# Nine output stores of a convolution move from ScalarE's instruction stream to SyncE's

## The chip, the cores and the metric

The kernel runs on one core of one Trainium2 chip. The metric is the device time of one launch, in microseconds (us). A core has a matrix engine (TensorE, PE in the profile), a vector engine (VectorE, DVE), an activation engine (ScalarE, ACT), a general engine (GpSimd, POOL) and SyncE (SP), which only issues transfers here. All five run their own instruction streams in order and meet at semaphores. Transfers (DMAs) are issued from SyncE, ScalarE or GpSimd, each of which has a queue of its own, and are carried out by 16 DMA engines.

## The reference

A causal convolution over 7 positions, with one softmax-normalised kernel per head, is followed by a mixture of experts with a capacity limit:

```python
# _attn_ref: x (8, 3584, 192), weight (8 heads, 7)
w = np.exp(weight - np.max(weight, axis=-1, keepdims=True))
w = w / (np.sum(w, axis=-1, keepdims=True) + 1e-09)
x_pad = np.concatenate([np.zeros((B, 6, D)), x], axis=1)
out = np.einsum('hk,bskhg->bshg', w, x_unf)        # 24 channels per head
# _moe_ref: N = 28672 tokens, D = 192, E = 8 experts, F = 1024, cap = N // E = 3584
logits = x @ w_gate
# tokens go to experts in falling order of logit, one expert each, while the expert has room
for e in range(E):
    mask = assigned == e
    out[mask] = np.maximum(x[mask] @ w1[e], 0.0) @ w2[e]
```

## The kernel before

The first stage, some 155 us, is the convolution. The input is cut into 16 *half batches* of 1792 positions. For each, `load` (line 183) brings the input into one of four buffers `X` of 118 partitions. It does so in three DMAs: the *head* (6 partitions, line 189 or 192), the *lower half* (112 partitions, 8 rows of 192 floats each, line 194 on SyncE) and the *upper half* (the same size, line 194 on ScalarE). SyncE issues the head and the lower half. The upper half is put on a list, `later`, and ScalarE issues it in the middle of a convolution, at the sixth of its eight heads. At the start of convolution i, `load(i + 3)` is written.

`conv` (line 202) does one half batch. For each of 8 heads TensorE multiplies the input by a banded matrix of the head's weights, into one of four PSUM banks `cv`, and ScalarE copies the bank to one of three output buffers `a`. This copy is called the eviction here. At the end the *store* (line 214) writes the output buffer, 1344 KB, to the array `attn` in the chip's memory. Before the change ScalarE issues it, at its place between the last eviction of one half batch and the first of the next.

The same half batch is then transposed by VectorE (`aT<-a`), TensorE forms the gate's logits from it (`pl`), ScalarE copies them out twice (`L<-pl`, `LT<-pt`), and VectorE takes the largest per token (`M<-LT`). This is one to two half batches behind the convolution. In between stand the steps of the routing, as a background list: a threshold search over the logits of the first half batches, then the counts and positions of the tokens of the first eight (half batches 0 to 7), among them a small copy on ScalarE called `tot`. From the lists that come out, GpSimd gathers the experts' first tokens from `attn`. The expert stage then runs to the end of the kernel, and TensorE has work for all of it.

The order of every engine's stream is fixed when the program is built. An estimate of the engines' progress (`Pace`, `Steps`) decides where the background steps are put; DMA issues count nothing in it. Waits are set by the builder, in two kinds that matter here:

- A wait for data or a free buffer: an eviction into `a` needs the store of three half batches earlier to have landed; a head needs TensorE to be done with the input of four half batches earlier.
- A wait for a semaphore. The DMAs of SyncE and ScalarE share eight completion semaphores (DMAHW0 to DMAHW7 in the listings), given out in turn. A DMA waits until the one that held its semaphore before has landed.

The routine of lines 1648 to 1680 is the loop over the half batches.

Of the kernel before, what the change touches and what calls it, by code (L numbers as in the profile page):

```python
# [114 lines left out]
def build(ctx, tc, nc, x, weight, wg, attn, LT, wk):  # L115
# [4 lines left out]
    V, A, PE, P = nc.vector, nc.scalar, nc.tensor, nc.gpsimd  # L120
# [81 lines left out]
    def conv(i, mid, hold=None):  # L202
        t = X.pop(i)
        a = AA[i] = k.ap[i % 3].tile([128, 16, D], F32, name="a")
        o = a.rearrange("p w (h c) -> p h w c", c=24)
        for h in range(8):
            ps = k.cps.tile([128, 512], F32, name="cv")
            PE.matmul(ps[:, 0:384], TH[0:118, h], t[:, :, h * 24:(h + 1) * 24], start=True, stop=True)
            mid(h)
            A.activation(o[:, h], ps[:, 0:384].rearrange("p (w c) -> p w c", c=24), AF.Copy)  # L210
        put = partial(A.dma_start, attn[i * 1792:(i + 1) * 1792].rearrange("(g p b) d -> p g (b d)", g=4, b=4),
                      a[0:W].rearrange("p (g b) d -> p g (b d)", b=4))
        if hold is None:
            put()  # L214
        else:
            hold.append(put)
# [24 lines left out]
    def logits_t(i):  # L241
# [5 lines left out]
        A.activation(o, v, AF.Copy)  # L247

    k.load, k.conv, k.transp, k.logits, k.logits_t = load, conv, transp, logits, logits_t
    k.toeplitz, k.gate_load, k.gate_ops = toeplitz, gate_load, gate_ops  # L250
    return k
# [1517 lines left out]
```

## Time and profile before

| | us |
|---|---|
| median of 3 runs (lowest to highest) | 1238.71 (1238.25 to 1239.27) |
| the profiled execution, whole | 1242.89 |
| its span | 1241.1 |
| TensorE busy in the span | 1203.0 (97%) |
| first store issued / last store issued | 21.23 / 156.44 |
| bytes moved by DMA over the span | 182.00 MB |

The profile is of one execution. Times in it count from the span's start. A row of a timeline gives the start, the length, the engine, the line, what is written from what, and in brackets how long the engine had stood idle before and what ended that wait. A row "ACTq" or "SPq" is the issue of a DMA by ScalarE or SyncE, not the transfer; its length is the time that the engine stood in it. Nearly all compute instructions pass through one helper, so their line is 56 and they are told apart by the names of their tiles.

### The profile page before, as it was taken

The numbers are of one execution on the slowest core, as the hardware profiler recorded it, in microseconds if no ns is written. First come the engines' busy times: TensorE is split into PE (matmuls) and PEld (weight loads), VectorE is DVE, ScalarE is ACT, GpSimd is POOL, SyncE is SP. The second block draws the span as 40 slices with busy tenths as digits, with TensorE's granted clock in tenths as the row PEclk, the third lists the DMA queues.
The fourth block names the chain that finished last, engine by engine and source line by source line (L and its number), as shares of the span: only waits on it lengthen the run. The fifth ranks groups of instructions, "written<-read, shape, count | busy, mean of one in ns | idle before, by whom it ended". The sixth has DMA issues, their size and how long they took to land.

```text
span 1241.1 us, 21785 instructions
## 1 busy us (share of the span) xinstructions
PE 1203.0 (97%) x7694; PEld 1033.9 (83%) x7694; DVE 984.8 (79%) x2126; ACT 559.6 (45%) x1251; POOL 532.5 (43%) x520
## 2 busy tenths in 40 slices
PE   6999899999999999999999999999999999999997
PEld 3545578889989988889888889999999999999996
DVE  7588679898998988889879856777777777777762
ACT  5544555556445454444554443343333433333332
POOL 2000234435556555555465435434544444543422
PEclk9999999999999999999999999999999999999999
DMA  9999664659427473745343442114223232423100
GB/s 249 369 347 325 202 215 121 151 159 323 140 68 215 134 244 83 255 155 184 102 130 105 126 106 70 45 39 158 94 100 105 100 101 93 155 69 125 48 24 28
DMA packets 128580, 182.00 MB, mean 147 GB/s; under 512 B 20992, under 2 KB 91088, under 8 KB 126800
## 3 DMA queue, kind: packets, MB, share of 16 engines
q1 hardware_dynamic: 85856, 104.13, 27.6%
q0 software_dynamic: 21504, 44.07, 12.0%
q10 hardware_dynamic: 21104, 32.34, 7.6%
q8 instruction: 62, 1.02, 0.3%
q14 instruction: 54, 0.44, 0.1%
HBM read 102.37 MB, written 78.12 MB: 145 GB/s over the span
## 4 chain that ended last, share of the span: by engine, by line
PE 87%; DVE 5%; DMA 4%; issue 1%; ACT 1%; ACTq 0%; SPq 0%; POOL 0%; POOLq 0%; DVEq 0%
PE ph L56 40%; PE y L56 39%; PE cv L56 4%; PE bg L56 3%; DMA attn<-a 3%; DVE X L56 1%; PE pl L56 1%; DVE TH L56 1%; DVE aT L56 1%; DVE hl L56 1%; DMA X<-otab 0%; PE px L56 0%; DMA wb<-in_weight_dram 0%; ACTq L214 0%; DMA otab<-X 0%
## 5 line engine op out<-in xcount | busy, mean ns | idle before, releaser
L56 PE MATMUL y<-w,hh 128*128 128x384 f32 x1792 | 535.7, 355 | 0.0
L56 ACT ACTIVATE hh<-ph 128x512 fp32r<-128x512 f32 x448 | 267.3, 597 | 453.1 <-PE ph L56 380.3
L56 PE MATMUL y<-w,hl 128*128 128x192 f32 x1792 | 448.9, 251 | 0.0
L56 DVE SCALAR_TENSOR_TENSOR hl<-ph,hh 128x512 fp32r<-128x512 f32 x448 | 307.6, 687 | 129.1 <-ACT hh L56 99.7
L56 PE MATMUL ph<-xa,w 128*128 128x512 f32 x1344 | 395.2, 402 | 0.4 <-DVE hl L56 0.4
L56 PEld LDWEIGHTS y<-w,hl 128*128 128x128 f32 x1792 | 340.9, 190 | 16.2
L56 PEld LDWEIGHTS y<-w,hh 128*128 128x128 f32 x1792 | 336.3, 188 | 20.9 <-issue 3.0
L1383 POOL DMA_INDIRECT out_dram<-yo,ia x128 | 144.3, 1127 | 240.2 <-DVE yo L56 195.7
L56 PEld LDWEIGHTS ph<-xa,w 128*128 128x128 f32 x1344 | 218.5, 189 | 21.6 <-issue 1.8
L1383 POOL DMA_INDIRECT out_dram<-yo,ib x96 | 94.9, 988 | 221.0 <-DVE yo L56 213.6
L56 PE MATMUL ph<-xd,w 128*128 128x512 f32 x448 | 177.3, 396 | 0.0
L1308 POOL DMA_INDIRECT xg<-attn,ja x128 | 141.5, 1106 | 78.9 <-issue 39.1
L56 PE MATMUL ph<-xd,dl 128*128 128x512 f32 x448 | 174.1, 389 | 0.2 <-issue 0.2
L56 DVE STREAM_TRANSPOSE xs<-xg 32x128 f32<-32x128 f32 (+2 forms) x408 | 164.8, 404 | 6.6
L56 ACT ACTIVATE yt<-y 128x192 f32<-128x192 f32 x224 | 73.0, 326 | 109.8 <-PE y L56 72.3
L56 DVE TENSOR_TENSOR yo<-y,yt 128x192 f32<-128x192 f32 x224 | 79.2, 354 | 49.9 <-ACT yt L56 46.6
L1308 POOL DMA_INDIRECT xg<-attn,jb x96 | 103.3, 1076 | 29.3 <-issue 29.3
L56 PE MATMUL cv<-X,TH 118*128 118x384 f32 x256 | 99.7, 516 | 13.9 <-DVE TH L56 12.2
L56 PEld LDWEIGHTS ph<-xd,dl 128*128 128x128 f32 x448 | 84.2, 188 | 20.1 <-issue 0.5
L56 PEld LDWEIGHTS ph<-xd,w 128*128 128x128 f32 x448 | 84.0, 187 | 19.6 <-issue 0.6
L56 PEld LDWEIGHTS cv<-X,TH 118*128 118x128 f32 x256 | 44.9, 195 | 43.7 <-POOL TH L152 12.0
L56 ACT ACTIVATE a<-cv 128x384 f32<-128x384 f32 x128 | 59.4, 493 | 43.1 <-PE cv L56 21.3
(237 smaller groups left out, 919.8 us busy)
## 6 DMA issues: line engine op xcount, KB each, us to landing
attn<-a ACTq DMA_DIRECT2D x16, 1344.0 KB
raw<-in_moe_w_dram SPq DMA_DIRECT2D x56, 192.0 KB
X<-in_x_dram SPq DMA_DIRECT2D x15, 672.0 KB
X<-in_x_dram ACTq DMA_DIRECT2D x15, 672.0 KB
kw<-w SPq DMA_DIRECT2D x36, 256.0 KB
kv<-w SPq DMA_DIRECT2D x24, 384.0 KB
scr<-xs SPq DMA_DIRECT2D x96, 96.0 KB
w<-kw SPq DMA_DIRECT2D x6, 1536.0 KB
```

Source lines behind the costliest of these rows:

```text
L56: return f(*a, **k)
L1308: self.nc.gpsimd.indirect_dma_start(out=t[:, b], out_offset=None, in_=self.attn[0:rows], in_offset=bass.IndirectOffsetOnAxis(ap=idx[b], ax ...
L1383: st = self.nc.gpsimd.indirect_dma_start(out=self.out, out_offset=bass.IndirectOffsetOnAxis(ap=idx, axis=0), in_=o, in_offset=None, bounds ...
```

## The change

The stores of half batches 0 to 8 are issued by SyncE and no longer by ScalarE. Those of 9 to 15 stay on ScalarE. What is stored, and from where, is the same.

```diff
@@ -208,7 +208,7 @@
             PE.matmul(ps[:, 0:384], TH[0:118, h], t[:, :, h * 24:(h + 1) * 24], start=True, stop=True)
             mid(h)
             A.activation(o[:, h], ps[:, 0:384].rearrange("p (w c) -> p w c", c=24), AF.Copy)
-        put = partial(A.dma_start, attn[i * 1792:(i + 1) * 1792].rearrange("(g p b) d -> p g (b d)", g=4, b=4),
+        put = partial((nc.sync if i < 9 else A).dma_start, attn[i * 1792:(i + 1) * 1792].rearrange("(g p b) d -> p g (b d)", g=4, b=4),
                       a[0:W].rearrange("p (g b) d -> p g (b d)", b=4))
         if hold is None:
             put()
```

The streams of TensorE, VectorE and GpSimd are the same in both programs. The first place is SyncE's stream while half batches 2 to 4 are convolved. X_451, X_519 and X_590 are the inputs of half batches 6, 7 and 8; a_387, a_455 and a_526 the outputs of 2, 3 and 4. Before:

```order
L189 DMA X_451<-in_x_dram 6x15x192 [waits DMAHW0_49,DMAHW5_49,PE_49,Pool_49]
L194 DMA X_451<-in_x_dram 112x8x192 [waits DMAHW7_49]
L192 DMA X_519<-in_x_dram 6x16x192 [waits DMAHW3_49,DMAHW1_49,PE_49]
L194 DMA X_519<-in_x_dram 112x8x192 [waits DMAHW3_49]
L189 DMA X_590<-in_x_dram 6x15x192 [waits DMAHW5_49,DMAHW6_49,PE_49,Pool_49]
L194 DMA X_590<-in_x_dram 112x8x192 [waits DMAHW7_49]
```

and now:

```order
L214 DMA attn_62<-a_387 112x4x768 [waits DMAHW7_49,Activation_49]
L189 DMA X_451<-in_x_dram 6x15x192 [waits DMAHW0_49,DMAHW2_49,PE_49,Pool_49]
L194 DMA X_451<-in_x_dram 112x8x192 [waits DMAHW2_49]
L214 DMA attn_62<-a_455 112x4x768 [waits DMAHW3_49,Activation_49]
L192 DMA X_519<-in_x_dram 6x16x192 [waits DMAHW5_49,DMAHW4_49,PE_49]
L194 DMA X_519<-in_x_dram 112x8x192 [waits DMAHW6_49]
L214 DMA attn_62<-a_526 112x4x768 [waits DMAHW7_49,Activation_49]
L189 DMA X_590<-in_x_dram 6x15x192 [waits DMAHW0_49,DMAHW1_49,PE_49,Pool_49]
L194 DMA X_590<-in_x_dram 112x8x192 [waits DMAHW2_49]
```

A store that waits for ScalarE's last eviction now stands ahead of each head and lower half, and the semaphores fall to other DMAs. In the new program DMAHW7 at store 2 was held by the upper half of half batch 5, and DMAHW2 at the lower half of half batch 6 by the upper half of 6. From the input of half batch 7 and the store of 3 on, each lower half and each store takes the semaphore of its own kind from two half batches earlier, until the stores are back on ScalarE.

The second place is ScalarE's stream between half batches 5 (a_594) and 6 (a_667). Before:

```order
L214 DMA attn_62<-a_594 112x4x768 [waits DMAHW2_49,Activation_49]
L56 ACTIVATE a_667<-cv_668 128x16x24 [waits DVE_49,PE_49]
L56 ACTIVATE a_667<-cv_673 128x16x24 [waits PE_49]
L56 ACTIVATE a_667<-cv_688 128x16x24 [waits PE_49]
L56 ACTIVATE a_667<-cv_692 128x16x24 [waits PE_49]
```

and now:

```order
L56 ACTIVATE a_594<-cv_650 128x16x24
L56 ACTIVATE a_667<-cv_668 128x16x24 [waits DVE_49,DMAHW3_49,PE_49,Activation_49]
L56 ACTIVATE a_667<-cv_673 128x16x24 [waits PE_49]
L56 ACTIVATE a_667<-cv_688 128x16x24 [waits PE_49]
L56 ACTIVATE a_667<-cv_692 128x16x24 [waits PE_49]
```

The store is gone from the stream, and with it the wait for the landing of store 3 (DMAHW2). That wait now stands at the first eviction of half batch 6 (DMAHW3), which writes the buffer that store 3 reads.

## The prediction

> **What bounds the kernel now.** I read the page first: the busy shares, and the shares of the chain of waits.
>
> ```profile
> PE 1203.0 (97%) x7694; PEld 1033.9 (83%) x7694; DVE 984.8 (79%) x2126; ACT 559.6 (45%) x1251; POOL 532.5 (43%) x520
> PE 87%; DVE 5%; DMA 4%; issue 1%; ACT 1%; ACTq 0%; SPq 0%; POOL 0%; POOLq 0%; DVEq 0%
> ```
>
> TensorE carries 87% of the chain. The experts' matmuls, which fill the time after about 155 us, touch none of the moved stores. So the change can only pay or cost in the first eighth, the convolution, and what it saves there goes on to the end, since TensorE has no slack behind it to soak it up. Next I cut that stage into windows (columns: stretch, length, then busy us of PE, PEld, DVE, ACT, POOL with instructions, clock, DMA share, GB/s).
>
> ```profile
> 20.00:57.00 37.00, 36.68 (x280) 19.40 (x279) 19.51 (x30) 20.83 (x53) 2.96 (x10) 1.00 1.07 356
> 57.00:92.00 35.00, 32.13 (x268) 16.75 (x267) 31.40 (x86) 16.77 (x46) 0.54 (x2) 1.00 1.07 349
> 104.00:138.00 34.00, 33.67 (x356) 22.74 (x356) 28.34 (x61) 18.58 (x44) 0.37 (x1) 1.00 0.96 305
> ```
>
> From 20 to 57 us TensorE is full (36.7 of 37). From 57 to 92 three things are nearly full at once: TensorE (92%), VectorE (90%, the first threshold search runs there) and the DMA engines (share over 1 at 349 GB/s). From 104 on TensorE is full again and the DMA share falls below 1. So there is idle TensorE time only between 57 and 104, and the chain of waits shows what it hangs on there (start, length, what):
>
> ```profile
> 74.48 17.52 DMA attn<-a
> 92.03 0.04 issue
> 92.07 3.76 ACTq L214
> ...
> 96.42 0.08 ACT tot L56
> 96.50 0.05 issue
> 96.55 0.41 PE bg L56 x4
> ```
>
> The store of half batch 7 takes 17.5 us to land. The store of half batch 9 (L214 at 92.07) is issued just behind that landing and holds ScalarE for 3.76 us. Then ScalarE's small copy of the totals comes late, and TensorE waits for it. ScalarE's own timeline shows the same at every store:
>
> ```profile
> 57.57 2.71 ACTq L214 DMA_DIRECT2D attn<-a  x1
> 74.48 3.11 ACTq L214 DMA_DIRECT2D attn<-a  x1
> 82.98 3.88 ACTq L214 DMA_DIRECT2D attn<-a  x1
> 86.96 2.02 ACT L56 ACTIVATE a<-cv 128x384 f32<-128x384 f32 x5 [4.28 <-PE bg L56]
> 92.07 3.76 ACTq L214 DMA_DIRECT2D attn<-a  x1
> 95.93 0.49 ACT L56 ACTIVATE a<-cv 128x384 f32<-128x384 f32 x1 [4.00 <-DVE aT L56]
> 96.32 0.17 ACT L56 ACTIVATE tot<-bg 128x8 bf16<-128x8 f32 x1
> ```
>
> The wait names PE or DVE, but those were done long before: ScalarE stood in the issue of the DMA. An unhindered issue takes 0.3 us; these take 2.7 to 3.9 us because ScalarE's queue is full.
>
> **The change, step by step.** Nine stores leave ScalarE's order and stand in SyncE's, each in front of the head and lower half of a later input. No arithmetic moves. What the 3 to 4 us cost today is not their sum, since four PSUM banks let TensorE run ahead. The cost is in the rows where TensorE itself stood still (and the ScalarE and VectorE rows beside them):
>
> ```profile
> 38.23 0.49 ACT L56 ACTIVATE a<-cv 128x384 f32<-128x384 f32 x1 [0.93 <-PE cv L56]
> 40.74 0.22 ACT L56 ACTIVATE L<-pl 128x64 f32<-128x64 f32 x1 [2.02 <-DMA X<-in_x_dram]
> 41.22 0.33 PE L56 MATMUL pt<-ident,L 128*128 128x128 f32 x1 [0.32 <-ACT L L56]
> 78.23 1.56 PE L56 MATMUL cv<-X,TH 118*128 118x384 f32 x4 [0.55 <-ACT a L56]
> 87.50 1.56 PE L56 MATMUL cv<-X,TH 118*128 118x384 f32 x4 [1.04 <-ACT a L56]
> 93.84 0.89 PE L56 MATMUL cv<-X,TH 118*128 118x384 f32 x2
> 96.55 0.40 PE L56 MATMUL bg<-U,tot 128*128 128x128 bf16 x4 [1.59 <-ACT tot L56]
> 91.58 0.38 DVE L56 TENSOR_REDUCE M<-LT 128x16 f32<-128x128 f32 x1 [2.13 <-ACT LT L56]
> ```
>
> *First*, 0.32 us at 41.2: ScalarE had stood 2.02 us at the issue of an upper input half, because the semaphore that this DMA takes over was still held by store 1. In the new order that half waits for an older load instead. *Second*, 0.55 + 1.04 = 1.59 us at 78.2 and 87.5, right behind the stores of half batches 7 and 8. The M<-LT row shows that both, with the first, lie on the path: VectorE stood idle 2.13 us there for the logits of half batch 7, more than the 1.91 us by which they come sooner. *Third*, the copy of the totals: the convolution that ScalarE must evict before it ends on TensorE at 93.84 + 0.89 = 94.73. Without the blocked issue that eviction starts about 94.8 instead of 95.93, 1.14 us sooner, and the copy and TensorE follow. This third store stays on ScalarE, but its queue then holds only upper input halves, so I take its issue at 0.3 us. The stalls sum to 0.32 + 1.59 + 1.14 = **3.05 us**. This is the gain if nothing replaces them.
>
> Next, what the stores meet in SyncE's order. The bytes do not change, and the engines that move them are busy throughout:
>
> ```profile
> q10 hardware_dynamic: 5641, 8.46, 69.3%
> q1 hardware_dynamic: 4941, 3.71, 37.3%
> attn<-a ACTq DMA_DIRECT2D x4, 1344.0 KB
> X<-in_x_dram SPq DMA_DIRECT2D x5, 672.0 KB
> X<-in_x_dram ACTq DMA_DIRECT2D x4, 672.0 KB
> X<-in_x_dram SPq DMA_DIRECT2D x3, 72.0 KB
> ```
>
> These are the queues between 57 and 92 us (packets, MB, share) and the sizes of the issues. A half batch moves 1344 + 672 + 672 + 72 KB, 2.83 MB. At the 349 GB/s of that window this takes 8.09 us; the stores at 57.57 and 92.07 are four half batches apart, 8.63 us each. So the DMA engines have 0.53 us to give per half batch, 4 x 0.53 = **2.1 us** over the stretch in which the gain arises, against the 3.05 us that the stalls would return. Input that lies ready can cover some of the difference, for the four input buffers are loaded ahead; the stores cannot, with three output buffers. ScalarE carries two thirds of the bytes today (8.46 of 12.21 MB). After the change SyncE carries 2088 of 2760 KB, three quarters. The two queues share by packets, not by bytes (5641 and 4941 packets here, for 69% and 37% of the time), so the light queue is served early and the heavy one late: upper halves will land before they are needed, stores a little later than now.
>
> The Trainium skill says the same of the hardware, in DMA: Bandwidth & Descriptors, section Issuing engines are not separate DMA queues: DMAs of all issuing engines run on the same 16 DMA engines and interleave, and issuing from several saves only issue time, "usually small relative to the DMA itself". The trace agrees on the first part by its share of 1.07; by the 3.9 us above the issue time is not small here.
>
> A late store is waited for by ScalarE in a new place. In the new order the first eviction into an output buffer waits itself for the store of three half batches ago; before, ScalarE had done that wait at a store's issue. At 74.48 + 17.52 = 92.00 the landing of store 7 was already the last thing before store 9's issue. That gives the bounds for a store's landing after the change: if it lands as now, at 92.0, the eviction of half batch 10 (due about 92.8 when TensorE is 1.91 us ahead) loses nothing; if it lands 3 us later, it starts at 95.0 and only 0.9 of the 3.05 us is left by that row. I take the nearer bound for the landing and let the DMA engines cap the gain: **2.1 us**, between 0.9 and 3.05.
>
> The other costs are about nothing. Nine SyncE issues of 0.3 us come on a queue that mostly sleeps. SyncE's wait for the last eviction delays a head by some 0.6 us, because that head waits anyway for TensorE to finish the same half batch. If SyncE's queue is full (it is at times now, 2.46 us at 49.22), its block falls on loads with a reserve. That reserve can be read: the lower half of half batch 10 takes the semaphore of the one of 8, so 8 had landed by 68.82, 5.7 us before store 7 is issued and convolution 8 begins.
>
> ```profile
> 36.88 0.57 SPq L194 DMA_DIRECT2D X<-in_x_dram  x1
> 53.82 0.31 SPq L194 DMA_DIRECT2D X<-in_x_dram  x1
> 68.82 0.31 SPq L194 DMA_DIRECT2D X<-in_x_dram  x1
> 49.22 2.46 SPq L189 DMA_DIRECT2D X<-in_x_dram  x1
> 131.48 0.63 ACT L56 ACTIVATE w<-raw 128x512 fp32r<-128x512 f32 x1 [0.47 <-DMA raw<-in_moe_w_dram]
> ```
>
> At the stage's end the first weights are loaded behind the last input. The row at 131.48 shows ScalarE waiting for them already, by 0.47 us, with TensorE full. In the new order the last of these loads waits for store 12, not 11, but store 12 is issued sooner too. I take no cost; if they come no sooner than now, roughly 1 us of the gain is left.
>
> The sum against the profiled execution: span 1241.1 - 2.1 = 1239.0 us, with the 1.8 us around it 1240.8. That execution (1242.89) lies 4.2 us above the median, so the median goes from 1238.71 to **1236.6 us**.
>
> **Rivals.**
> *All of it returns.* If the reserve of loaded input covers what the DMA engines lack, and stores land no later, 3.05 us come back: 1235.7; with store issue and load blocks both gone, down to 1233.8. For it: 5.7 us of reserve. Against: the DMA share of 1.07 leaves nothing idle.
>
> *The wait moves.* Stores land 3 us later in the heavy queue and ScalarE waits at the eviction as long as it now stands in the issue. Then the 1.59 and 1.14 us stay, and 0.32 is left: 1238.4. For it: store 7 was on the chain with no room at all. Against: ScalarE's block today begins after that landing and adds 3.76 us to it; a wait in its place would have to be as long.
>
> *SyncE's order is too stiff, slower.* In the old order SyncE's stream holds only loads. In the new one, the lower half of half batch 6 stands behind store 2 and waits for the semaphore of upper half 6, which ScalarE issues about 38.7, behind the eviction of the row at 38.23. That lower half was issued at 36.88, and had landed by 53.82, 16.9 us later. Say the upper half takes 8 us: then the lower half goes at 47 and, with the same 16.9, lands at 64, while convolution 6 starts at 57.6. TensorE would stand 6.4 us, less the 2.1 gained: 1238.71 + 4.3 = 1243.0. The point from which it decides is a landing later than about 62.2 (57.6 + 2.1 + the 2.5 us that can be told). Against: much less is queued on SyncE when it has been held back, so 16.9 us is a far bound; at half of it the input lands at 55.5, in time.
>
> The Trainium skill speaks for this rival, in Perfetto Trace Analysis, section DMA Optimizations: it may help to give one DMA-capable engine the inputs and another the outputs. Neither order here does so; no run here shows a clean separation.
>
> **How the numbers follow.** A difference under 0.2%, 2.5 us, cannot be told from none in this kernel. The forecast (gain 1.2 to 2.9, 1235.8 to 1237.5) has 0.42, of which 0.15 lies beyond the 2.5 us. All of it returning: 0.25, faster. The wait that moves, gain 0 to 1.2: 0.16, same. SyncE too stiff: 0.17, of which 0.02 ends within 0.2%. So faster 0.15 + 0.25 = 0.40; same 0.27 + 0.16 + 0.02 = 0.45; slower 0.15. The range runs from the full return, 1233.8, to a mild form of the last rival, 1240.6. The likeliest's own range is 1235.8 to 1237.5.
>
> **What would show it.** In the profile after: L214 under SyncE nine times, with issues of 2 us and more there; no ScalarE issue over 1 us before 100 us; the rows "PE cv <- ACT a" near 78 and 87 gone or under 0.5 us; the totals' copy near 94 instead of 96.3; ScalarE waiting for a DMA of attn at the first eviction of a half batch, up to some 2 us. Wrong would be: TensorE waiting for input at 48 to 60 us (the stiff order); a copy of the totals at 96 or later (the wait has moved); or DMA well over 349 GB/s between 57 and 92 (then the cap was no cap).

## The result, and where the time went

The changed kernel takes **1250.35 us** (median of 5 runs, 1248.49 to 1251.92) against 1238.71 before: a ratio of **1.0088, 95% interval 1.0075 to 1.0102**, slower by 11.6 us. The forecast was 1236.6, and its range ended at 1240.6. The profiled execution after took 1249.44 us with a span of 1247.6. That span is only 6.5 us above the one before, because the expert stage of the profiled execution before was some 4 us slow (it lay 4.2 us above its median, as the prediction said). The stage with the stores is compared directly.

The page first: the busy shares hardly move, but DMA rises from 4% to 5% of the chain of waits (PE is TensorE's share there, 87% as before).

```profile
PE 1205.7 (97%) x7694; PEld 1035.4 (83%) x7694; DVE 986.0 (79%) x2126; ACT 562.2 (45%) x1251; POOL 532.8 (43%) x520
PE 87%; DVE 5%; DMA 5%; issue 1%; ACT 1%; POOL 0%; POOLq 0%; DVEq 0%; ACTq 0%
```

TensorE's stream is the same in both kernels, so its rows serve as mile posts: one in the convolution of half batch 10, the end of that of 12, and a step of the routing (`bg<-iq,ones`) behind that of 13. The last row of each is the issue of store 15 by ScalarE. Before:

```profile
98.59 1.56 PE L56 MATMUL cv<-X,TH 118*128 118x384 f32 x4
122.67 0.81 PE L56 MATMUL cv<-X,TH 118*128 118x384 f32 x2
134.59 0.27 PE L56 MATMUL bg<-iq,ones 128*128 128x256 bf16 x1
156.44 0.31 ACTq L214 DMA_DIRECT2D attn<-a  x1
```

After:

```profile
94.03 0.17 ACT L56 ACTIVATE tot<-bg 128x8 bf16<-128x8 f32 x1
96.30 1.56 PE L56 MATMUL cv<-X,TH 118*128 118x384 f32 x4
124.47 0.81 PE L56 MATMUL cv<-X,TH 118*128 118x384 f32 x2
145.22 0.28 PE L56 MATMUL bg<-iq,ones 128*128 128x256 bf16 x1
166.89 0.31 ACTq L214 DMA_DIRECT2D attn<-a  x1
```

In half batch 10 the change is 2.29 us *ahead*: the gain that was forecast is there (the totals' copy is at 94.03, before 96.32). At the end of convolution 12 it is 1.80 behind, so 4.09 us were lost, and at the step of the routing it is 10.63 behind, another 8.83. Store 15 is 10.45 us late. TensorE's timeline after shows the stalls that do it:

```profile
101.74 1.53 PE L56 MATMUL cv<-X,TH 118*128 118x384 f32 x4 [1.71 <-DMA X<-in_x_dram]
106.37 1.56 PE L56 MATMUL cv<-X,TH 118*128 118x384 f32 x4 [0.46 <-ACT a L56]
114.28 1.53 PE L56 MATMUL cv<-X,TH 118*128 118x384 f32 x4 [2.24 <-DMA X<-in_x_dram]
138.31 1.65 PE L56 MATMUL cv<-X,TH 118*128 118x384 f32 x2 [6.28 <-ACT a L56]
```

The first is input 11, the third input 12; with the second they are 4.41 us, close to the 4.09. The fourth names ScalarE, but ScalarE was waiting itself, for the first expert weights, in front of the evictions that TensorE needed:

```profile
136.76 0.63 ACT L56 ACTIVATE w<-raw 128x512 fp32r<-128x512 f32 x1 [8.65 <-DMA raw<-in_moe_w_dram]
```

The chain of waits says why the weights were late, in two rows that follow each other: the load is issued when store 11 has landed, because it takes over that store's semaphore.

```profile
113.09 11.00 DMA attn<-a
124.10 12.55 DMA raw<-in_moe_w_dram
```

SyncE's timeline after, from input 11 on (L194 the lower halves 11, 12 and, as the third, 15; L214 store 8; L1235 the first weight load):

```profile
89.08 0.34 SPq L194 DMA_DIRECT2D X<-in_x_dram  x1
89.52 0.52 SPq L214 DMA_DIRECT2D attn<-a  x1
...
103.83 0.31 SPq L194 DMA_DIRECT2D X<-in_x_dram  x1
...
119.06 1.53 SPq L194 DMA_DIRECT2D X<-in_x_dram  x1
124.10 0.35 SPq L1235 DMA_DIRECT2D raw<-in_moe_w_dram  x1
```

and the same three loads before (lower half 11, lower half 12, first weights):

```profile
76.71 0.31 SPq L194 DMA_DIRECT2D X<-in_x_dram  x1
84.11 0.31 SPq L194 DMA_DIRECT2D X<-in_x_dram  x1
112.80 0.85 SPq L1235 DMA_DIRECT2D raw<-in_moe_w_dram  x1
```

They are issued 12.4, 19.7 and 11.3 us later than before. At the last stall a second cost shows, in the windows (length, PE busy, ..., granted clock, DMA share, GB/s):

```profile
132.00:136.00 4.00, 0.03 (x1) 0.00 (x0) 0.00 (x0) 0.00 (x0) 0.00 (x0) 1.00 0.89 332
136.00:140.00 4.00, 1.70 (x5) 0.92 (x6) 2.58 (x4) 3.24 (x7) 0.00 (x0) 0.61 0.32 113
140.00:144.00 4.00, 4.00 (x21) 2.96 (x20) 3.09 (x5) 2.85 (x6) 0.00 (x0) 0.53 0.60 166
```

Late in the idle stretch the granted clock falls to half, for about 6.9 us (4 x 0.39 + 4 x 0.47 = 3.44 us lost, twice that in length), until some 143.8. Of that, 5.4 us lie behind the end of the stall at 138.31, in which half the work, 2.7 us, is lost. Of the 8.83 us, 6.28 are the stall, and the remaining 2.55 are about this.

### The profile page after: what moved, and what is told of

It reads as the page before. It is cut to its first block, busy times and chain, and to the rows that moved or that the text cites. A ratio compares the mean times of both kernels' runs of the same rounds, so it can differ in the third digit from the quotient of the medians.

```text
span 1247.6 us, 21789 instructions
## 1 busy us (share of the span) xinstructions
PE 1205.7 (97%) x7694; PEld 1035.4 (83%) x7694; DVE 986.0 (79%) x2126; ACT 562.2 (45%) x1251; POOL 532.8 (43%) x520
## 4 chain that ended last, share of the span: by engine, by line
PE 87%; DVE 5%; DMA 5%; issue 1%; ACT 1%; POOL 0%; POOLq 0%; DVEq 0%; ACTq 0%
PE ph L56 40%; PE y L56 39%; PE cv L56 4%; DMA attn<-a 4%; PE bg L56 2%; PE pl L56 1%; DVE X L56 1%; DMA raw<-in_moe_w_dram 1%; DVE hl L56 1%; DVE aT L56 1%; DVE oa L56 0%; DVE TH L56 0%; PE px L56 0%; DVE sl L56 0%; DMA wb<-in_weight_dram 0%
## 5 line engine op out<-in xcount | busy, mean ns | idle before, releaser
L56 PE MATMUL cv<-X,TH 118*128 118x384 f32 x256 | 102.2, 526 | 24.0 <-DVE TH L56 12.0
```

Of the source, the lines that this page charges most:

```text
L56: return f(*a, **k)
```

## The experiments

My theory when the runs were planned: what costs is the *handover*, the place where stores 9 and later are back on ScalarE while SyncE still carries store 8 and the input, together with the shared semaphores, which fall to other kinds of DMAs there. The rivals: the DMA engines are too full for the loads whatever the order; the stores on SyncE cost as such, by their number. The runs were made on several chips, on which the kernel before had medians from 1228.82 to 1242.43 us; so each ratio is to before on the same chip, and times are compared through the ratios.

**The weights off SyncE, and a control.** The first six weight loads are issued by GpSimd, once in the changed kernel and once in the one before.

```diff
+        q_ = nc.gpsimd if self.loaded < 4 else nc.sync
-            nc.sync.dma_start(t, self.w1[e, 0:128, s])
+            q_.dma_start(t, self.w1[e, 0:128, s])
...
```

> The changed kernel, with the first six loads of expert weights issued by GpSimd, outside SyncE's stream and its eight semaphores. Theory (SyncE's order at the handover): the first weight load no longer stands behind input 15 and store 11, ScalarE's 8.65 us at w<-raw go, TensorE's 6.28 us stall near 138 goes with the 2.5 us or so that the half clock behind it costs: 1250.35 - 8.8 = 1241.5 us, 1239 to 1244 (the stalls for X near 102 and 114, 1.71 + 0.46 + 2.24 us, stay). Rival (the DMA engines are too full for the loads, whatever the order): the weights come late all the same, 1248 or more. Rival (the stores on SyncE as such): little moves, 1247 or more.

> Control: the kernel before, with the same six weight loads issued by GpSimd. Theory: the weights were in time there (TensorE full from 104 to 138), so 1238.7 us within 1.5. If GpSimd's issue itself gains or loses something, it shows here, and the other run is read against this one. Rival (DMA engines too full): six loads sooner crowd out the input, 1241 or more.

Measured: after_gpw 1236.92 us, ratio 1.0059 (1.0037 to 1.0081); before_gpw 1227.75, 0.9988 (0.9975 to 1.0001). The control came out as expected: loads on GpSimd cost nothing there. The other did not. The wait at the weights is gone, but the loss has moved to input 12, where after_gpw has these rows in TensorE's timeline and in the windows:

```profile
118.36 2.90 PE L56 MATMUL cv<-X,TH 118*128 118x384 f32 x4 [6.33 <-DMA X<-in_x_dram]
```

```profile
116.00:120.00 4.00, 1.64 (x3) 1.07 (x4) 0.41 (x1) 0.00 (x0) 0.00 (x0) 0.55 1.10 303
...
128.00:132.00 4.00, 4.00 (x28) 2.12 (x30) 3.62 (x11) 1.47 (x3) 0.00 (x0) 0.50 0.54 105
```

The stall of 6.33 us is followed by half clock until 132 at least. The weight loads, issued from 100 us, had gone ahead of lower half 12, which SyncE issued at 103.73. So this run speaks for the rival with the full DMA engines as far as input 12 goes. It is also no clean test of the weights, since by their new place they delay that input: lower half 12 landed at 114.15 after and at 118.22 here.

**Fewer stores, another engine.** Six stores on SyncE instead of nine (thr6), and stores 0 to 8 on GpSimd (store_pool).

```diff
-        put = partial((nc.sync if i < 9 else A).dma_start, ...
+        put = partial((nc.sync if i < 6 else A).dma_start, ...      # thr6
+        put = partial((P if i < 9 else A).dma_start, ...            # store_pool
```

> Six stores on SyncE (0 to 5) instead of nine; the handover lies three half batches sooner, and the semaphores fall otherwise: the first weight load takes over that of lower input 13, no store's; but lower input 9 takes over that of store 6, on ScalarE. Theory (order and shared semaphores at the handover): the weights come in time, no stall near 138, no clock dip; instead TensorE waits for input 9 near 84 to 92, since store 6 lands about 82 and a lower half takes about 11 us: 5 to 10 us, so 1241 to 1249, with the loss at another place. Rival (the number of stores on SyncE as such): two thirds of the loss, about 1246.5, at the same places as with nine. Rival (DMA engines too full): stalls near 102, 114 and 138 as with nine.

> Stores 0 to 8 issued by GpSimd instead of SyncE: off ScalarE, but not in SyncE's stream and not on its semaphores. Theory: ScalarE's blocked issues go (the 3.05 us of the prediction), the loads keep their order, the weights come as before: 1235.5 to 1238. Rival (a store ahead of loads is what hurts, on whatever engine, for want of bandwidth): 1242 or more.

Measured: thr6 1238.09, ratio 1.0071 (1.0046 to 1.0095); store_pool 1235.9, 1.0053 (1.0036 to 1.0069). TensorE's stalls in thr6:

```profile
77.20 1.53 PE L56 MATMUL cv<-X,TH 118*128 118x384 f32 x4 [3.44 <-DMA X<-in_x_dram]
89.95 2.90 PE L56 MATMUL cv<-X,TH 118*128 118x384 f32 x4 [3.29 <-issue]
```

They are at inputs 8 and 9, three half batches sooner, as the handover is. (The second row names "issue", but lower half 9, which took over the semaphore of store 6, landed at 89.86, just ahead of it.) ScalarE does not wait for weights at all here. The place of the loss goes with the handover, which the rivals do not say. Whether lower half 9 is late by the queues or because it had to wait for store 6 (it was issued only at 78.66), this run does not separate. store_pool refutes what I expected of it. It has no store in SyncE's stream, but TensorE waits for input at 33.8, 54.4 and 82.1 us, and for GpSimd:

```profile
44.56 1.53 PE L56 MATMUL cv<-X,TH 118*128 118x384 f32 x4 [2.96 <-POOL irep L325]
...
82.12 1.53 PE L56 MATMUL cv<-X,TH 118*128 118x384 f32 x4 [2.98 <-DMA X<-in_x_dram]
```

GpSimd's own work (`irep`) now stands behind a store that waits for an eviction, and the loads land late although only loads stand in their stream. Lower half 8, for instance, was issued at 60.39 and landed at 81.99, 21.6 us later. So a store beside the loads can make them late through the DMA engines alone.

**The semaphore of input 12 alone.** One small load, the head of input 12, goes to GpSimd. This shifts the semaphores behind it by one: lower half 12 is no longer bound to store 9. The changed kernel itself ran beside it on the same chip; in a third kernel the weights are on GpSimd as well.

```diff
+        hq = P if i in (12,) else nc.sync
-            nc.sync.dma_start(t[0:6, 1:16], ...
+            hq.dma_start(t[0:6, 1:16], ...
...
```

> The changed kernel itself, on the chip of the runs beside it, so that these can be read against it. All theories: ratio to before 1.008 to 1.010.

> The changed kernel, with one small load (the head of input 12, 72 KB) issued by GpSimd. It leaves SyncE and, what counts, shifts the semaphores behind it by one: the lower half of input 12 takes over that of lower half 10 (landed 89.7) instead of store 9 (103.8). Theory (semaphores at the handover): that half is issued near 90 to 92 instead of 103.83, TensorE's 2.24 us stall for input 12 near 114 goes; the first weights are still behind store 11 in part and keep most of their stall. So 2 to 5 us less than after, ratio 1.005 to 1.007. Rival (the DMA engines are too full at that place, whatever the order): the half lands near 114 all the same and crowds out another load, ratio 1.008 to 1.010 as after.

> The same with the first six weight loads also issued by GpSimd: now neither input 12 nor the weights stand behind a store. Run after_gpw lost 6.33 us at input 12 and as much again to the half clock behind it. Theory (order and semaphores): both stalls go, the dip of the clock goes with them; what stays is input 11 (about 1.7 us) and an eviction (about 1 us) against 2.3 us gained up to 100: ratio 0.999 to 1.003. Rival (DMA engines too full): input 12 stays late beside the weights, ratio 1.005 or more.

Measured: after_again 1253.38, ratio 1.0087 (1.0062 to 1.0112); after_h12 1253.09, 1.0077 (1.0055 to 1.0099); after_gpw_h12 1254.58, 1.0101 (1.0078 to 1.0123). The second is not told apart from the first by its interval, the third is worse than I expected. In after_h12 lower half 12 was issued at 90.52 instead of 103.83, as meant, but it landed at 113.29, and at 114.15 before the shift:

```profile
90.52 2.34 SPq L195 DMA_DIRECT2D X<-in_x_dram  x1
```

In after_gpw_h12 it was issued at 90.52 as well and landed at 116.83, and TensorE stood 2.90 us for it. This **refutes the semaphore of store 9 as the cause of input 12's delay**: issued 13 us sooner, the half landed 0.86 us sooner, as the rival with the full DMA engines had said, and 1.0101 lies in that rival's range too. (TensorE's stall for input 12 is gone in after_h12 all the same. It came to that input only at 113.43, because the copy of the totals had cost it 2.24 us; store 7 landed at 95.15 there, not at 93.54.) What was issued before it has to pass first. The queues of the kernel after between 92 and 104 us show what that is (packets, MB, share):

```profile
q1 hardware_dynamic: 1437, 2.07, 52.5%
q10 hardware_dynamic: 1457, 2.17, 50.1%
```

ScalarE's queue (q10) has store 9 in it; SyncE's (q1) has lower half 11, store 8 and head 12. Over the 12 us both moved about as much. The Trainium skill states a rule for this, in DMA: Bandwidth & Descriptors, section Queues, rings and completion order: a DMA engine goes round the queues that have work, one packet from each at a time. The trace agrees only in part. From 96 to 101 us, with store packets on both queues, they moved 426 (q1) and 405 packets; from 92.2 to 95.5 it was 747 to 267, and from 101.5 to 104 117 to 653. What the landings show does not hang on the rule: store 9, issued by ScalarE at 90.46, landed at 103.81, ahead of store 8, which SyncE had issued 0.94 us sooner and which landed at 105.72. So the store on the light queue overtakes what is on the heavy one; two stores run at once in front of input 12.

**No handover in the input.** Twelve stores on SyncE, with the weights on GpSimd (thr12_gpw); all sixteen (thr16_gpw); twelve with the weights left on SyncE (thr12).

```diff
-        put = partial((nc.sync if i < 9 else A).dma_start, ...
+        put = partial((nc.sync if i < 12 else A).dma_start, ...     # thr12, thr12_gpw
+        put = partial((nc.sync if i < 16 else A).dma_start, ...     # thr16_gpw
```

> Twelve stores on SyncE instead of nine, so that the handover to ScalarE lies behind the last wait of an input for a store's semaphore, and the six weight loads on GpSimd. Theory (what costs is the handover, not the stores on SyncE): no wait of an input half for a store, input 11 late by at most 2 us, ratio 0.998 to 1.002. Rival (stores on SyncE cost by their number, for they stand in the loads' order and queue): twelve cost more than nine, ratio 1.008 or more.

> Twelve stores on SyncE as in thr12_gpw, but the weight loads left on SyncE: the pair tells what the weights' place in SyncE's stream costs by itself, without the handover. In this order the first weight load stands behind store 11 and the halves of input 15, the last of which takes over the semaphore of upper half 15. Theory (the weights' place is a term of its own, some 6 us of stall and up to 7 us of half clock): first weight load issued at 128 or later, ScalarE waits at w<-raw for over 4 us, ratio 1.004 to 1.010. Rival (late weights are only a consequence of the handover, which is gone here): w<-raw waits under 1.5 us, ratio 0.999 to 1.003 as thr12_gpw.

> All sixteen stores on SyncE, six weight loads on GpSimd: no handover at all. Theory (the handover costs, where a store on ScalarE's queue and one on SyncE's run side by side ahead of the input): as thr12_gpw, ratio 0.999 to 1.003. Rival (stores on SyncE cost by their number): 1.004 or more.

Measured: thr12_gpw 1243.66, ratio **1.0007** (0.9992 to 1.0022); thr12 1251.66, **1.0095** (1.0071 to 1.0120); thr16_gpw 1232.5, 1.0030 (1.0012 to 1.0048). These three settle most of it. thr12_gpw differs from after_gpw only in the engine of stores 9 to 11, and the loss is gone: store 9 is now behind lower half 12 on SyncE. Lower half 11 landed at 98.63 and 12 at 111.49, against 103.64 and 116.83 in after_gpw_h12, 5 us sooner. That is near what 1344 KB take at that stage's rate (1.376 MB at the 343 GB/s that thr12_gpw moves from 57 to 92 us, 4.0 us). With the weights on SyncE in both, after and thr12 show the same: lower half 11 landed at 101.60 and 99.05, lower half 12 at 114.15 and 106.98. So the handover is a cause. That it acts by overtaking fits the landings; that no other semaphore than store 9's has a part in it is not shown. Twelve stores on SyncE cost less than nine here (1.0007 against 1.0059), so the rival that counts them falls for these. It is not settled beyond: sixteen took 1.0030, and with the weights on SyncE six, nine and twelve gave 1.0071, 1.0087 and 1.0095, whose intervals overlap.

thr12 differs from thr12_gpw only in the weights' place, and pays 8.8 parts in a thousand for it. TensorE has no stall over 1 us up to 128 us, and then this:

```profile
138.83 1.65 PE L56 MATMUL cv<-X,TH 118*128 118x384 f32 x2 [10.71 <-ACT a L56]
```

```profile
137.28 0.63 ACT L56 ACTIVATE w<-raw 128x512 fp32r<-128x512 f32 x1 [13.09 <-DMA raw<-in_moe_w_dram]
```

Here the first weight load is issued at 129.14, behind a lower half 15 that waited for upper half 15 to land (128.76). It takes over no store's semaphore; it is late because of what stands ahead of it in SyncE's stream. So the weights are a second cause by themselves. Only the two changes together bring the loss down to nothing (1.0059 and 1.0101 with the weights alone moved off SyncE, 1.0095 with the handover alone gone). So the two prices do not add. I read this as each delay taking time in which the other would have been waited for; in part it is also that the weights on GpSimd delay input 12 themselves. thr16_gpw has no stall for input over 0.35 us, but TensorE waits once for the gather that reads the stored rows; why that gather is late there I did not follow up.

```profile
148.93 0.47 PE L56 MATMUL bg<-ident,xg 128*128 128x128 f32 x1 [3.56 <-DMA xg<-attn,ja]
```

**The rate of the DMA engines from 20 to 57 us.** All kernels with stores off ScalarE move fewer bytes there. Before and after, in the view of the DMA queues:

```profile
DMA packets 11565, 13.19 MB, mean 356 GB/s; under 512 B 258, under 2 KB 9626, under 8 KB 11561
```

```profile
DMA packets 10621, 11.81 MB, mean 319 GB/s; under 512 B 236, under 2 KB 8974, under 8 KB 10617
```

1.38 MB less, half of a half batch's traffic. I thought that store 2 was held back on SyncE by a semaphore (it is issued at 43.35, before at 34.15) and that loads moving alone are slow. The head of input 4 goes to GpSimd, which shifts that semaphore; once in the changed kernel, once in thr12_gpw, with the same diff as for input 12.

> The changed kernel, with one small load (the head of input 4, 72 KB) issued by GpSimd. That shifts the semaphores by one just there: store 2 takes over that of store 0 (landed 32.7) and not that of upper half 5 (43.3), and with it stands on SyncE from about 36 instead of 43.35. Theory (waits for taken-over semaphores hold early stores back, the DMA engines meanwhile move loads alone at 275 GB/s, and the reserve is gone by the handover): 335 to 355 GB/s from 20 to 57 us instead of 319 to 330, store 3 to 5 land 1 to 3 us sooner, input 11 is not late any more; the weights stay late: ratio 1.003 to 1.007. Rival (the lower rate comes from stores and upper halves in two queues as such): 319 to 330 GB/s as before, ratio 1.007 to 1.010.

> Twelve stores on SyncE, six weight loads and the head of input 4 on GpSimd. Theory as for after_h4: thr12_gpw came out even (1.0007) with 327 GB/s from 20 to 57 us; with that rate at 335 to 355 it is faster than before, ratio 0.997 to 0.9995. Rival (two queues as such): 1.000 to 1.002, rate as there.

Measured: after_h4 1239.57, ratio 1.0076 (1.0054 to 1.0098); thr12_gpw_h4 1228.4, 0.9990 (0.9980 to 0.9999). Their windows:

```profile
20.00:57.00 37.00, 35.72 (x275) 18.50 (x274) 20.19 (x34) 19.66 (x50) 3.84 (x11) 1.00 1.08 319
```

```profile
20.00:57.00 37.00, 36.98 (x281) 19.70 (x280) 19.96 (x31) 21.56 (x54) 3.83 (x11) 1.00 1.06 334
```

319 in after_h4 is the rival's number, 334 in the other just misses mine; store 2 was issued at 38.44 and 37.40. So that semaphore is not what lowers the rate, or a small part of it. That loads alone are slow the trace does show: in the kernel after, these are a stretch in which nearly all packets are loads (92.2 to 95.5) and one with store packets among them (101.5 to 104):

```profile
DMA packets 1014, 0.83 MB, mean 250 GB/s; under 512 B 22, under 2 KB 986, under 8 KB 1014
```

```profile
DMA packets 770, 0.96 MB, mean 384 GB/s; under 512 B 20, under 2 KB 603, under 8 KB 770
```

Why they run alone for longer once the stores share SyncE's queue stays open. With rates of 327 and 334 GB/s, also below the 356 before, thr12_gpw and thr12_gpw_h4 come out even or 0.1% faster, so by itself it costs little there. thr12_gpw_h4 beats both kernels by its interval, by a hair; before_gpw, which moves no store at all, comes to the same 0.9988.

**The same stall, two prices.** after_again is the changed kernel itself, in another execution. Its stall for input 12 is no longer than in the profile of after (2.00 us against 2.24), but what follows is another thing:

```profile
113.87 2.23 PE L56 MATMUL cv<-X,TH 118*128 118x384 f32 x4 [2.00 <-DMA X<-in_x_dram]
```

```profile
116.00:120.00 4.00, 4.00 (x44) 2.95 (x44) 0.26 (x1) 0.49 (x1) 0.00 (x0) 0.50 1.09 289
...
124.00:128.00 4.00, 4.00 (x28) 2.08 (x27) 3.90 (x10) 1.00 (x5) 0.00 (x0) 0.50 0.97 199
```

```profile
116.00:120.00 4.00, 4.00 (x62) 2.79 (x53) 0.43 (x1) 0.83 (x2) 0.00 (x0) 1.00 1.09 291
```

TensorE ran at half clock from about 115 to 128 in the one execution (upper rows) and at full clock in the other (last row, the profile of after). In after_again TensorE then came to the weights so late that it hardly waited there (1.00 and 1.23 us near 140), though half clock followed again, from about 142 to 149. The totals agree, 1.0088 and 1.0087.

## Why the prediction was wrong

**The gain was right.** The three stalls went: no issue of ScalarE's takes over 0.32 us from 20 to 100 us, the waits near 78 and 87 are 0.28 us and gone, and the copy of the totals came at 94.03, 2.29 us sooner, where 3.05 was the sum of the stalls and 2.1 was taken. The third stall gave less than its 1.14: TensorE still waited 0.81 us for that copy, of 1.59 before.

**The landing of a store** was put between 92.0 and 95.0. Store 7 landed at 93.54, and the eviction that waits for it stood 3.22 us, instead of up to 2; with ScalarE freed this still left the 2.29 us.

**SyncE's full queue** was foreseen, and its price was not. Its store issues took up to 5.78 us, and the loads behind them had the reserve that I read off near 69 us. That reserve held up to input 10 (TensorE waited 0.19 us for input at 56.66 and no more until 101). I carried it on to the end of the stage, where it was used up. None of the signs that would have shown the forecast wrong came either (no wait of note at 48 to 60, the copy at 94.03, 348 GB/s from 57 to 92): all three looked at times before 97 us, and the loss came after.

**The step that failed** is the one on the stage's end: "the last of these loads waits for store 12, not 11, but store 12 is issued sooner too. I take no cost". It followed the last weight load. ScalarE meets the *first* one, in front of its evictions, and that had moved from behind upper half 13 to behind store 11 and input 15: 0 was taken, some 1.1 us of the 2.1 allowed as the bound, and 8.83 us came of it, the clock included. thr12 shows this as a cause of its own, at 1.0095.

**What was not in the sum** is the handover. The text said that the light queue is served early and the heavy one late, but drew this only for upper halves and not for store 9, which is a store on the light queue ahead of input 11 and 12 on the heavy one. It cost 4.09 us in the profile of after, and thr12_gpw against after_gpw and after_gpw_h12 shows it. That the queues share by packets, on which this rested, the trace bears out only in part (426 to 405 packets in one stretch, 747 to 267 in another).

**The rivals.** "SyncE's order is too stiff, slower" had the right side and the right kind, late input and first in line a wait behind a taken-over semaphore. It was put at input 6, where 0.19 us was lost, and priced at 1243.0; the loss is at inputs 11 and 12 and at the weights. "All of it returns" and "the wait moves" fall. The DMA cap on the gain (2.1 us) agrees with the 2.29 in size, and the rate that it was worked out from held (348 GB/s from 57 to 92, before 349). That the cap is the reason is not shown: the gain is a little above it, and the rate from 20 to 57 fell to 319, a stretch that the cap leaves out. The working for the stiff order, with upper half 6 at 38.7 and its lower half at 47, came out (38.56 and 47.66), and the input landed in time but for the 0.19 us, as the rival's nearer bound had it.

## What to carry to other kernels

Where a transfer changes its issuing engine for a part of a loop, follow it to the place where it changes back, and past the loop's end to the first load that an in-order engine meets there: ask of that load what stands ahead of it in its stream and whose semaphore it takes over. A transfer on the lighter of two queues can overtake what waits on the heavier one, as store 9 did, so moving stores to balance issue time can make the input late. And price a stall of TensorE above its length: the slower clock behind it can double it.

## What the runs showed of the hardware

A stall of TensorE may be followed by half clock for longer than the stall itself: 6.33 us were followed by some 15 us of it in one run (after_gpw), 2.00 us by some 13 us in another (after_again), 1.44 us by about 7 us (thr12_gpw, 0.55 and 0.59 from 112 to 120). 6.28 us were followed by only 5.4 us (the half clock had begun 1.4 us before the stall's end), and 2.24 us by none (both after). The Trainium skill, in TensorE: Matmul & The Clock Gate, Part 1, tells of a free-running window: the clock is halved after at least one idle window of about 3.4 us. The trace agrees in so far as the same stall can end either way, but not on the length: 2.00 us was enough, and 1.44 us.

That a store issued 0.94 us later on the lighter queue lands 1.9 us sooner than one on the heavier (after), and that loads alone move at 250 GB/s and loads beside stores at 384 (after), I had not expected to matter as they did. One small load of 72 KB moved to another engine changes which DMA waits for which behind it: in after_h12 lower half 12 was issued at 90.52 instead of 103.83.
